# Fewer w4 products in the early attention units, output tiles seven units behind, sums by DMA for all but one unit

## The chip, the cores and the metric

The kernel runs on one core of a Trainium2 chip. The metric is the device time of one execution in microseconds. The kernel before takes 199.26 us, the median of three runs (198.9 to 199.65). The engines are named as in the profile: PE multiplies matrices, DVE, ACT and POOL work elementwise, SP only issues DMAs (ACT and POOL can issue them too). Every engine, and every queue of DMA issues, works in its own order: what stands behind a waiting instruction waits with it.

## The reference

An input `x` of 2048 rows by 512 columns in bf16 is normalized by rows and goes two ways; the output is `x + s * g`.

```python
xn = _layernorm(x)
s = _A_ref(xn, A_wqkv, A_wo)      # attention: 32 heads of 16, each row sees itself and rows 2, 4, ... 14 before it
g = _silu(_B_ref(xn, B_w1, B_w2, B_w3, B_w4))
...
    x1 = x + hs                   # hs: gelu(layernorm(x) @ w1), shifted by rows in four groups of columns, @ w2
    h2 = _gelu(_layernorm(x1) @ w3) @ w4
    return x1 + h2
```

The attention's weights are a softmax over 8 logits; the kernel takes exponentials without a maximum, sums them, and divides the weighted values by the sums afterwards. `w3` is 512 by 1376 and `w4` 1376 by 512.

## The kernel before

**Layout.** Since attention looks back by even distances, even and odd rows never meet there; they are two parities `p` of 1024 rows each. Until about 104 us the kernel normalizes, forms queries and keys, and does w1, w2 and w3. What is left is the *attention part*, which the change is about. There PE has four kinds of work:

- 17 *attention units*: unit 0 for the first 64 rows of both parities, then eight units of 120 rows for each parity. `scores(n)` (line 603) fills four PSUM banks, `exps(n)` (L614, ACT) takes exponentials, `within(n)` (L623, DVE) masks them in place, `values(n)` (L582) makes the value rows of the unit in the bank called b, which ACT copies (L587), and `weighted(n)` (L650) multiplies masked exponentials by values, with a column of constants that yields the sums. Its two banks o are emptied by DVE at the edge between the unit's two halves (`mix` L666, L667) and by ACT for the rest (L668), into a tile `orw`.
- 16 *w4 tiles* of 128 rows, `w4_part` (L529), 11 products each into the one bank w, then an add of x1 on DVE (L537) that also frees the bank.
- Gates: silu of a w4 tile, as `tanh` of half of it (ACT, L555, same function table as the exponentials) and a multiply (`gate_mult`, DVE, L561). At the end, after the last exponentials, ACT loads the table of silu and takes it directly (L547); such tiles are scaled by 2 later (`twice`), which is what the tanh form leaves in.
- 16 *output tiles* of 128 rows, `final(p, i)` (L802): attention rows `oT` by wo into a bank, DVE multiplies by the gate (L813, or L811 for tiles in `twice`), POOL adds x (L818), and SP stores two tiles at once (L844).

**Sums.** Units form *runs* that share the division. A run of two units spans 240 rows. `sums_gather` reads the sums out of `orw` by two DMAs (L679), `sums_invert` takes the reciprocal on DVE (L757) and writes it to DRAM (L759), `sums_read` reads it back spread over rows (L765), `moves` copies the weighted values into `oT` by eight DMAs (L693), and `sums_apply` multiplies (L773). The constant NC is 3: the last four units are runs of their own. Unit 13 goes by DMA like the others, with its apply on POOL. Units 14, 15 and 16 go through PE instead: `sums_turn` transposes the sums (L703), `sums_inverse` takes the reciprocal on DVE (L711) and expands it in two ACT copies (L716), `sums_back` transposes back (L741), `sums_mult` multiplies (L750). For units 15 and 16 `rows` also brings the weighted values to `oT` by PE (L728) and ACT (L733).

**Order.** The order on each engine is the order of the source; nothing is reordered. In unit n (0 to 15) the loop issues scores(n), weighted(n-1), exps(n), the eviction, values(n+1), the gates of earlier tiles, the DMAs of the runs, the mask, w4 tile n, the output tile due and the applies due. Output tile (p, i) is due in unit 6 + 8p + i, up to (1, 1) in unit 15. Unit 15 takes six of the 11 products of its w4 tile (`CUT`). The end, written out by hand, holds unit 16, five products of w4 tile 15 and an identity product (L535), output tiles (1, 2) to (1, 7), and the sums of three units between them. Tiles (1, 6) and (1, 7) take their add of x on PE (`pe_add`, L835 and L838, ACT copies the result, L839); (1, 7) works in two halves, the last half stored from ACT's queue.

Tiles are handed out from pools: `orw` and the exponentials share six buffers, xo (x for the output) has four, and from unit 10 the space of the queries of parity 0 is cut into sixteen `slots`.

## Time and profile before

| what | value |
|---|---|
| median of three runs | 199.26 us (198.9 to 199.65) |
| the profiled run | 199.36 us |
| its span | 197.6 us (197.64) |
| granted PE clock | 1.0 throughout |
| PE, ACT, DVE, POOL busy | 190.2, 126.7, 125.1, 61.8 us |
| attention part | from 103.3 us to the end |
| scores of unit 1 | 108.28 us |
| one unit, 1 to 5 | 4.32 us |
| one unit with an output tile, 6 to 14 | 5.18 us and some tenths in places |
| output tile (1, 7) begins | 191.96 us |
| last store issued by SP | from 193.10 us on |

The profile shows one execution. The span runs from the first instruction to the last; the device time lies a little above it. "The chain that ended last" follows the work back from the last instruction to what released each step. In the timeline a row gives start and length in us, the engine, the line of the kernel, and what was made from what; a bracket gives the time for which the engine was idle ahead of it and what ended that. Starts are what to compare on ACT and DVE, since the shown lengths of neighbours overlap by some 0.1 us.

### The profile page before, as it was taken

The numbers are of one execution on the slowest core, as the hardware profiler recorded it, in microseconds if no ns is written. First come the engines' busy times: TensorE is split into PE (matmuls) and PEld (weight loads), VectorE is DVE, ScalarE is ACT, GpSimd is POOL, SyncE is SP. The second block draws the span as 40 slices with busy tenths as digits, with TensorE's granted clock in tenths as the row PEclk, the third lists the DMA queues.
The fourth block names the chain that finished last, engine by engine and source line by source line (L and its number), as shares of the span: only waits on it lengthen the run. The fifth ranks groups of instructions, "written<-read, shape, count | busy, mean of one in ns | idle before, by whom it ended". The sixth has DMA issues, their size and how long they took to land.

```text
span 197.6 us, 6164 instructions
## 1 busy us (share of the span) xinstructions
PE 190.2 (96%) x2591; PEld 98.5 (50%) x2591; DVE 125.1 (63%) x249; ACT 126.7 (64%) x140; POOL 61.8 (31%) x114
## 2 busy tenths in 40 slices
PE   7699999999999999999999999999999999999991
PEld 2588844444444444444444555555555554546550
DVE  4788856418539968200004776788888887786892
ACT  3559849644830643556558788887666676667961
POOL 4135722810200220200000533032626242469760
PEclk9999999999999999999999999999999999999999
DMA  5982181389452256460330012222232271713333
GB/s 158 304 281 84 60 268 53 122 151 339 140 154 62 76 137 167 121 140 0 119 117 3 12 22 66 73 49 69 44 101 62 59 207 31 233 33 88 88 119 108
DMA packets 33643, 22.32 MB, mean 113 GB/s; under 512 B 17584, under 2 KB 33104, under 8 KB 33616
## 3 DMA queue, kind: packets, MB, share of 16 engines
q1 hardware_dynamic: 32256, 21.06, 37.5%
q0 software_dynamic: 1216, 0.81, 2.1%
q8 instruction: 20, 0.33, 0.7%
q10 hardware_dynamic: 144, 0.07, 0.1%
q14 instruction: 7, 0.06, 0.1%
HBM read 12.41 MB, written 4.83 MB: 87 GB/s over the span
## 4 chain that ended last, share of the span: by engine, by line
PE 91%; DMA 3%; DVE 2%; SPq 1%; issue 1%; ACT 1%; DVEq 0%
PE w_ps L529 19%; PE w_ps L394 18%; PE qk_ps L297 13%; PE v_ps L582 8%; PE w_ps L354 7%; PE w_ps L330 7%; PE wo_ps L802 6%; PE o_ps L650 6%; DMA wqk_sb<-in_A_wqkv_dram 3%; PE s_ps L603 3%; PE w_ps L410 1%; PE tr_ps L265 1%; SPq L118 1%; PE dt_ps L703 1%; DVE oT L750 1%
## 5 line engine op out<-in xcount | busy, mean ns | idle before, releaser
L614 ACT ACTIVATE prob<-s_ps 128x2048 bf16<-128x2048 f32 (+1 forms) x18 | 31.9, 1781 | 18.0 <-PE s_ps L603 17.9
L529 PE MATMUL w_ps<-w_sb,h3T 128*128 128x512 bf16 (+1 forms) x176 | 40.8, 379 | 0.0
L398 ACT ACTIVATE h3T<-w_ps 128x1024 bf16<-128x1024 f32 x20 | 20.5, 1023 | 24.9 <-PE w_ps L394 24.9
L693 POOL DMA_DIRECT2D oT<-orw x38 | 19.4, 518 | 49.9 <-DVE orw L658 30.3
L394 PE MATMUL w_ps<-x1nT,w_sb 128*128 128x512 bf16 x160 | 35.0, 379 | 0.0
L297 PE MATMUL qk_ps<-xnT,wqk_sb 128*128 128x256 bf16 (+1 forms) x192 | 29.7, 308 | 1.2 <-DMA wqk_sb<-in_A_wqkv_dram 0.7
L529 PEld LDWEIGHTS <-h3T 128*128 128x128 bf16 (+1 forms) x176 | 17.1, 98 | 20.4
L394 PEld LDWEIGHTS <-w_sb 128*128 128x128 bf16 x160 | 15.6, 98 | 19.1 <-issue 0.4
L297 PEld LDWEIGHTS <-wqk_sb 128*128 128x128 bf16 x192 | 18.3, 98 | 11.2 <-DMA wqk_sb<-in_A_wqkv_dram 1.0
L623 DVE TENSOR_TENSOR prob<-prob,band 128x2048 bf16<-128x2048 bf16 (+1 forms) x18 | 21.0, 1167 | 2.9 <-ACT prob L614 2.7
L304 ACT ACTIVATE qT<-qk_ps,sel 128x1024 bf16<-128x1024 f32 x16 | 16.7, 1113 | 6.6 <-PE qk_ps L297 6.5
L818 POOL TENSOR_TENSOR xo<-sg,xo 128x512 bf16<-128x512 bf16 x9 | 11.7, 1304 | 21.5 <-DVE sg L813 21.5
L802 PE MATMUL wo_ps<-wo_sb,oT 128*128 128x512 bf16 (+1 forms) x68 | 16.6, 366 | 0.1
L582 PE MATMUL v_ps<-wv_sb,xnT 128*128 128x512 bf16 x64 | 16.6, 381 | 0.0
L359 DVE TENSOR_TENSOR xn<-w_ps,xn 128x1024 bf16<-128x1024 f32 x8 | 9.7, 1212 | 10.6 <-PE w_ps L354 10.6
L537 DVE TENSOR_TENSOR xn<-w_ps,xn 128x512 bf16<-128x512 f32 x15 | 10.4, 691 | 7.6 <-PE w_ps L529 7.5
L585 DVE CAST v_aug<-v_ps 128x512 bf16<-128x512 f32 x1 | 0.7, 691 | 22.5 <-ACT h3T L398 22.5
L668 ACT ACTIVATE orw<-o_ps 128x896 bf16<-128x896 f32 x16 | 14.6, 913 | 0.1
L330 PE MATMUL w_ps<-xn2T,w_sb 128*128 128x512 bf16 x64 | 14.5, 379 | 0.0
L354 PE MATMUL w_ps<-w_sb,hT 128*128 128x512 bf16 x64 | 14.3, 379 | 0.0
L650 PE MATMUL o_ps<-prob,v_aug 64*32 64x64 bf16 x1088 | 12.2, 195 | 0.1
L334 ACT ACTIVATE hT<-w_ps 128x1024 bf16<-128x1024 f32 x8 | 8.2, 1028 | 6.2 <-PE w_ps L330 6.2
(100 smaller groups left out, 236.0 us busy)
## 6 DMA issues: line engine op xcount, KB each, us to landing
x1n_dram<-xn SPq DMA_DIRECT2D x4, 512.0 KB
xn<-in_A_x_dram SPq DMA_DIRECT2D x6, 256.0 KB
xo<-in_A_x_dram SPq DMA_DIRECT2D x6, 256.0 KB
out_dram<-xo SPq DMA_DIRECT2D x6, 256.0 KB
orw<-rden_d SPq DMA_DIRECT2D x6, 240.0 KB
w_sb<-in_B_w_dram SPq DMA_DIRECT2D x1, 1376.0 KB
w_sb<-in_B_w_dram SPq DMA_DIRECT2D x1, 1280.0 KB
wqk_sb<-in_A_wqkv_dram SPq DMA_DIRECT2D x2, 512.0 KB
```

What stands on the lines that cost most here:

```text
L297: pe.matmul(pt[:, b, :], lhsT=wqk_sb[:, dt, nt * P : (nt + 1) * P], rhs=xnT[p][:, dt, ms], start=(dt == 0), stop=(dt == ND - 1),)
L330: pe.matmul(pt[:, b, :], lhsT=w1_sb[:, dt, g * P : (g + 1) * P], rhs=xn2T[:, dt, :], start=(dt == 0), stop=(dt == ND - 1),)
L354: pe.matmul(pt[:, j, :], lhsT=w2_src(p, g, m0), rhs=w2_sb[:, g, :], start=(g == 0), stop=(g == ND - 1),)
L394: pe.matmul(pt[:, b, :], lhsT=w3_sb[:, dt, ft * P : (ft + 1) * P], rhs=x1nT[:, dt, :], start=(dt == 0), stop=(dt == ND - 1),)
L398: act.activation(h3_tile(c)[:, 2 * a : 2 * a + 2, :], pt, AF.Gelu_apprx_tanh)
L529: pe.matmul(pt, lhsT=h3[c][:fs, ft, jj * P : (jj + 1) * P], rhs=w4_sb[:fs, ft, :], start=(ft == 0), stop=(ft == NF - 1 and t < NN - 2),)
L582: pe.matmul(vp, lhsT=xnT[p][:, dt, k0 : k0 + P], rhs=wv_sb[:, dt, :], start=first, stop=last)
L614: act.activation(pr[:, rs_], t[:, rs_], AF.Exp, scale=SCALE)
L623: dve.tensor_tensor(out=w, in0=w, in1=b.unsqueeze(1).to_broadcast([P, m, KB]), op=ALU.min)
L650: pe.matmul(op[32 * cg : 32 * cg + 32, s, g * KB : (g + 1) * KB], lhsT=va[KB * s : KB * s + KB, dt * 8 + h, :], rhs=pr[KB * s : KB * s + K ...
L693: queues[hh % len(queues)].dma_start(out=oT[p][DH * hh : DH * (hh + 1), :, q0 : q0 + nq], in_=w[32 * cg : 32 * cg + DH, ND * jj : ND * jj ...
L802: pe.matmul(pt, lhsT=oT[p][:, dt, i * P : (i + 1) * P], rhs=wo_sb[:, dt, cs], start=(dt == 0), stop=(dt == ND - 1),)
```

## The change

Runs are now (0), then pairs up to (13, 14), then 15 and 16 alone, ten in all; NC is gone. Units 13, 14 and 15 have their sums by the DMA way, unit 16 alone through PE.

The w4 work is laid out by a table `part`: unit 0 takes tile 0, units 1 to 3 take tiles 1 and 2 (7, then 4 + 3, then 8 products), units 4 to 6 take tiles 3 and 4 likewise, unit n from 7 to 15 takes tile n - 2. In units 2 and 5, which end one tile and begin another, the first part stands ahead of values. Tiles 14 and 15 are left to the end. Output tiles are due in unit 7 + 8p + i, so seven, (1, 1) to (1, 7), are left to the end. Up to unit 6 the reciprocals and the reading back stand behind the mask. The first two applies come in unit 6 instead of 5. In units from 8 on SP issues four and POOL two of the six early moves of a run, instead of three and three.

At the end, the eviction of unit 15 goes to DVE, one of the two gathers of unit 15 is issued by ACT, four tiles (12 to 15) get silu directly instead of two, and the gate of output tile (1, 4) goes `through`: ACT copies the product out of PSUM in fp32 and doubles it, POOL multiplies by the gate and adds x.

```diff
-    NC = 3
-    runs = [(0, 0)] + [(a, a + 1) for a in range(1, NN - NC - 1, 2)] + [(a, a) for a in range(NN - NC - 1, NN)]
+    runs = [(0, 0)] + [(a, a + 1) for a in range(1, NN - 2, 2)] + [(a, a) for a in range(NN - 2, NN)]
...
-    def weighted(n, first=lambda: None):
+    def weighted(n, eng=act):
...
-        return lambda: act.activation(wide(ow, c, KB, m), wide(ov_, 0, CH + W, m), AF.Copy)
+        dst, src = wide(ow, c, KB, m), wide(ov_, 0, CH + W, m)
+        return lambda: act.activation(dst, src, AF.Copy) if eng is act else eng.tensor_copy(out=dst, in_=src)
...
-    def sums_gather(i):
+    def sums_gather(i, queues=[sp]):
...
-            sp.dma_start(
+            queues[j % len(queues)].dma_start(
...
+        def through(eng):
+
+            (cs, pt), = pts
+            o = slot(2).rearrange("p a d -> p (a d)").bitcast(F32)
+            act.activation(o, pt, AF.Copy, scale=2.0 if t in twice else 1.0)
+            sg = slot()
+            eng.tensor_tensor(out=sg, in0=o, in1=g_i, op=ALU.mult)
+            eng.tensor_tensor(out=x_o, in0=sg, in1=x_o, op=ALU.add)
...
-    final_at = {n: divmod(n - 6, 8) for n in range(6, 16)}
-    CUT = 6
+    final_at = {n: divmod(n - 7, 8) for n in range(7, 16)}
+    part = {0: [(0, 0, NF)]}
+    for n in (1, 4):
+        t = 1 + (n - 1) // 3 * 2
+        part.update({n: [(t, 0, 7)], n + 1: [(t, 7, NF), (t + 1, 0, 3)], n + 2: [(t + 1, 3, NF)]})
+    part.update({n: [(n - 2, 0, NF)] for n in range(7, NN - 1)})
     for i in range(0, 8, 2):
         load_xo(0, i)
     act.preload_act_table_set("exp_and_others")
     values(0)
     for n in range(NN - 1):
         scores(n)
-        back = [i for i, (a, b) in enumerate(runs) if b == n - 2 and i < R - NC]
+        back = [i for i, (a, b) in enumerate(runs) if b == n - 2]
         done = [i for i, (a, b) in enumerate(runs) if b == n - 1]
         evict = weighted(n - 1) if n > 0 else lambda: None
-        for i in back:
-            sums_invert(i)
+        if n > 6:
+            for i in back:
+                sums_invert(i)
         exps(n, 2 if n == 0 else 1)
-        if n == NN - 2:
+        evict()
+        gate_mult()
+        if len(part[n]) > 1:
+            w4_part(*part[n][0])
+        if n > 0:
             values(n + 1)
-        evict()
-        if 0 < n < NN - 2:
-            values(n + 1)
-        gate_mult()
         if n < NN - 2:
             gate_tanh()
         for i in done:
-            if i < R - NC:
-                sums_gather(i)
+            sums_gather(i)
         if n == 2:
             moves(0, [sp, pool], 1)
-        for i in back:
-            if 0 < i < R - NC - 1:
-                moves(i, [sp], None, [6, 7])
-            sums_read(i)
+        def read_back():
+            for i in back:
+                if i > 0:
+                    moves(i, [sp], None, [6, 7])
+                sums_read(i)
+        if n > 6:
+            read_back()
         for i in done:
             if i == 0:
                 moves(i, [sp, pool], 0)
-            elif i < R - NC - 1:
-                moves(i, [pool, sp], None, range(6))
-            elif i == R - NC - 1:
-                moves(i, [pool], None, range(4))
+            elif i == R - 3:
+                moves(i, [pool, sp])
             else:
-                moves(i, [pool, sp])
-        if n == NN - 2:
-            store(sp, 0, 6)
+                moves(i, [pool, sp] if n < 8 else [pool, sp, sp], None, range(6))
         within(n, 2 if n == 0 else 1)
-        late = [i for i, (a, b) in enumerate(runs) if n == max(b + 3, 5)]
-        w4_part(n, 0, NF if n < NN - 2 else CUT)
+        if n <= 6:
+            for i in back:
+                sums_invert(i)
+            read_back()
+        late = [i for i, (a, b) in enumerate(runs) if n == max(b + 3, 6)]
+        w4_part(*part[n][-1])
         if n == 0:
             values(n + 1)
         gate = final(*final_at[n]) if n in final_at else None
-        if n == NN - 2:
-            banks["end"] = True
-            sums_turn(R - 3, "o")
-            sums_inverse(R - 3)
-            for i in late:
-                sums_apply(i)
         if gate:
             gate(pool)
-        if n < NN - 2:
-            for i in late:
-                sums_apply(i)
-        if n == NN - 3:
-            moves(R - NC - 1, [pool], None, range(4, 8))
-        if n % 2 == 0 and 10 <= n < NN - 3:
-            load_xo((n - 2) // 8, (n - 2) % 8)
-        if n - 1 in final_at and n % 2 == 0 and n < NN - 3:
-            p, i = final_at[n - 1]
-            store(sp, p, i - 1)
-        if n in (10, 12):
-            load_xo(1, n - 6)
+        for i in late:
+            sums_apply(i)
+        if n in (10, 12, 14):
+            store(sp, 0, n - 10)
+        if n in (8, 10):
+            load_xo(1, n - 4)
+        if n in (12, 14):
+            load_xo(1, n - 12)
+    banks["end"] = True
     scores(NN - 1)
-    evict = weighted(NN - 2)
-    store(sp, 1, 0)
+    evict = weighted(NN - 2, dve)
+    sums_invert(R - 3)
     exps(NN - 1)
     evict()
+    sums_gather(R - 2, [sp, act])
+    sums_read(R - 3)
+    moves(R - 2, [pool], None, range(6))
     act.preload_act_table_set("silu_and_others")
-    w4_part(NN - 2, CUT, NF)
+    within(NN - 1)
+    w4_part(NN - 3, 0, NF)
+    for t in (NN - 5, NN - 4):
+        gate_silu(t)
+    sums_invert(R - 2)
+    moves(R - 2, [sp], None, range(6, 8))
+    sums_read(R - 2)
+    store(sp, 0, 6)
+    gate1 = final(1, 1, "b")
+    gate1(pool)
+    store(sp, 1, 0)
+    evict = weighted(NN - 1)
+    evict()
+    gate_silu(NN - 3)
+    layout("high", f=1, g=1, h=1, i=1)
+    final(1, 2, "f")(pool)
+    final(1, 3, "h")(pool)
+    store(sp, 1, 2)
+    w4_part(NN - 2, 0, NF)
     gate_silu(NN - 2)
-    within(NN - 1)
-    gate2 = final(1, 2, "b")
-    layout("high", f=1, g=1, h=1, i=1)
-    sums_back(R - 3, "f")
-    gate3 = final(1, 3, "h")
-    sums_apply(R - 4, pool)
-    evict = weighted(NN - 1, first=lambda: gate2(pool))
-    evict()
-    sums_turn(R - 2, "g")
-    sums_inverse(R - 2, rows(R - 2, "i"), True)
-    gate3(pool)
-    store(sp, 1, 2)
-    gate4 = final(1, 4, "w")
-    sums_mult(R - 3)
+    sums_apply(R - 3)
     sums_turn(R - 1, "g")
-    sums_back(R - 2, "f")
-    sums_inverse(R - 1, rows(R - 1, "h"), True)
-    sums_mult(R - 2)
-    gate_silu(NN - 3)
-    gate5 = final(1, 5, "b")
-    gate4(pool)
+    sums_inverse(R - 1, rows(R - 1, "i"), True)
+    gate4 = final(1, 4, "b")
+    gate4.through(pool)
+    sums_back(R - 1, "g")
+    sums_mult(R - 1)
+    sums_apply(R - 2)
+    gate5 = final(1, 5, "f")
     gate5(pool)
     store(sp, 1, 4)
-    sums_back(R - 1, "i")
-    gate6 = final(1, 6, "g")
-    sums_mult(R - 1)
+    gate6 = final(1, 6, "h")
     halves = [slice(0, D // 2), slice(D // 2, D)]
     add6 = pe_add(1, 6, "o", slice(0, D))
     gate6(None)
-    gate7 = final(1, 7, "fw", lambda: add6(gate6.sg))
+    gate7 = final(1, 7, "bw", lambda: add6(gate6.sg))
     store(sp, 1, 6, 1)
-    add7 = pe_add(1, 7, "h", halves[0])
+    add7 = pe_add(1, 7, "i", halves[0])
     gate7.mult(0)
     add7(gate7.sg)
     store(sp, 1, 7, 1, halves[0])
```

In the first line of this last part, `n - 6` becomes `n - 7`. Lines that start with a space are the same in both.

More of the change, by code (lines that the diff above doesn't have):

```diff
@@ L663, in weighted @@
         )
-        first()
         mix = small.tile([P, 2 * ND, W], F32, name="mix", tag="mix")
@@ L826, in gate @@
                     gate.add(eng)
+        def through(eng):
[5 more added lines that the diff above has]
+            eng.tensor_tensor(out=x_o, in0=sg, in1=x_o, op=ALU.add)
+        gate.through = through
         gate.mult = lambda k: mult(k, *pts[k])
```

## The prediction

> **What bounds the kernel now.** I read the busy shares, then the 40 slices, then the chain of waits in order of time, then the timeline of the attention part (from 104 us) engine by engine.
>
> ```profile
> PE 190.2 (96%) x2591; PEld 98.5 (50%) x2591; DVE 125.1 (63%) x249; ACT 126.7 (64%) x140; POOL 61.8 (31%) x114
> ...
> PE   7699999999999999999999999999999999999991
> ...
> PE 91%; DMA 3%; DVE 2%; SPq 1%; issue 1%; ACT 1%; DVEq 0%
> ```
>
> PE is the bound; the chain is PE work back to back. So products moved from one unit to another cost nothing by themselves, products removed gain their length, and a wait put ahead of PE loses its length. One early unit in the chain (start, length):
>
> ```profile
> 112.59 0.36 PE s_ps L603 x32
> 112.95 0.61 PE o_ps L650 x64
> 113.56 0.97 PE v_ps L582 x4
> 114.53 2.38 PE w_ps L529 x11
> ```
>
> ACT in the next unit, from the timeline (start, length, what it ran):
>
> ```profile
> 117.37 1.88 ACT L614 ACTIVATE prob<-s_ps 128x2048 bf16<-128x2048 f32 x1 [0.61 <-PE s_ps L603]
> 119.15 0.91 ACT L668 ACTIVATE orw<-o_ps 128x896 bf16<-128x896 f32 x1
> 119.94 0.60 ACT L587 ACTIVATE v_aug<-v_ps 128x512 bf16<-128x512 f32 x1
> 120.42 0.64 ACT L555 ACTIVATE sig<-xn 128x512 bf16<-128x512 bf16 x1
> ```
>
> A unit lasts 4.32 on PE: scores 0.36, weighted 0.61, values 0.97, eleven w4 products 2.38 (0.216 each). ACT starts one thing 1.78, 0.79 and 0.48 us after the last, and the tanh takes some 0.55: 3.05 without a tanh, 3.60 with one. An output tile is 0.86 on PE. Then three places of the timeline near the end, a reciprocal that waits for gathered sums (idle time before it in brackets), the last work of POOL and DVE, and the last SP stores:
>
> ```profile
> 174.12 0.53 DVE L757 RECIPROCAL rb<-dn 128x60 bf16<-128x60 bf16 x1 [0.55 <-DMA dn<-orw]
> ...
> 190.80 2.27 POOL L818 TENSOR_TENSOR slots<-slots 128x512 bf16<-128x512 bf16 x2 [1.40 <-PE wo_ps L802]
> 191.25 0.65 DVE L750 TENSOR_TENSOR oT<-rr_ps,oT 128x480 bf16<-128x480 f32 x1
> ...
> 193.10 1.68 SPq L844 DMA_DIRECT2D out_dram<-slots  x3
> ```
>
> The last three SP stores are issued back to back from 193.10, when POOL has added tiles 4 and 5 (190.80 + 2.27); the span ends 4.54 later, at 197.64. The profiled run took 199.36 with a span of 197.64, so 1.72 lies outside; the median of the runs shown is 199.26, 0.10 below. All sums below are made against 197.64 and 199.36. A measurement of this kernel tells about 0.5%, 1.0 us, from no change.
>
> **Units 1 to 15.** Up to the scores of unit 16, PE did 160 w4 products and ten output tiles from 108.28 to 181.21; afterwards 143 and nine. That moves 17 x 0.216 + 0.86 = 4.53 behind this point, which is then reached at 176.68 if nothing waits.
>
> Does anything wait? The six early units now hold 22 products per three units: 1.94 + 7 x 0.216 = 3.45, 3.45 and 3.67. Over six units PE needs 21.1, ACT 6 x 3.05 + 4 x 0.55 = 20.5: it fits, barely. The mask (L623) follows the exponentials: these start 0.57 after the scores, take 1.88, the mask 1.22, so weighted products can start 3.75 after the scores, where PE comes to them at 3.45 + 0.36 = 3.81. In units 2 and 5 one tile ends and the next begins in the same PSUM bank, and the add that frees it (L537, 0.69) stands ahead of the mask on DVE: mix and edge until 1.6, gate 2.2, add 2.9, mask 4.1. PE waits some 0.1 for the bank and 0.2 for the mask. That is 0.5 over both. So unit 16 starts at 177.2. The later units are as before (5.18 each, final tiles shifted by one); SP's extra move in each run falls in a queue that issues some 7 of every 10.4 us. The sums of runs 0 and 1 are applied one unit later, and the first output tile, which needs them, moves one unit later too.
>
> **From the scores of unit 16, taken as 0.** Removed: two transposes of sums (L703: 0.41 and 0.54), two transposes back (0.21 each), one row product (0.33): 1.70 of PE, and the 0.44 that PE waited at 181.62 for a reciprocal that held the bank of weighted. Also gone are four ACT expansions and two reciprocals from PSUM, hidden before. Added: two reciprocals by DMA, an eviction on DVE, two silus instead of tanhs, one gate sent through ACT and POOL.
>
> PE: scores 0.36, weighted(15) to 0.97, w4 tile 14 to 3.35, output (1,1) to 4.21. DVE meanwhile, in its order, by the times of unit 12: gate 0.18, apply 0.79, mix 1.35, edge 1.61, reciprocal of run 7 at 1.75. Its sums are gathered from -1.94 to -0.76. Such a gather was found landed 2.42 after its last issue (160.53 to 162.95) or waited for until 3.25 (170.87 to 174.12, behind two loads and a store). I take the first: one store and one load stand ahead here. Then the new eviction: between 0.91 (the same shape on ACT) and 1.23 (128x1024 on DVE); by elements of the DVE row 1.08. It ends at 3.2 and the mask of unit 16 at 4.4, so weighted(16) starts at 4.45: 0.24 of PE waiting.
>
> After it: two output tiles to 6.8, w4 tile 15 with its identity product to 9.4, transpose of sums 9.8, rows 10.1, output 4 to 11.0, back at 11.0 (reciprocal 0.36 and two expansions 0.72 after the transpose), output 5 to 12.1. Output 6 waits for the sums of run 8 on DVE: rows copied 11.5, multiply 12.15, apply 12.45. It runs from 12.5 to 13.4, 0.45 late. The DMA way of run 8 from the eviction at 3.2: gather issues 0.6, landing 2.4, reciprocal and issue 0.75, write to read 1.5 (123.91 to 125.41) to 2.1 (153.37 to 155.46), read issue 0.65, landing 2.33 (183.31 to 185.64): 11.5 to 12.1, just in time. Before, output 6 ended at 191.51; now 177.2 + 13.4 = 190.6: **PE is 0.95 earlier**.
>
> The stores are another matter. Output 4 now goes ACT copy (0.6, from 11.35), POOL multiply, POOL add, and only then comes POOL's add of output 5. SP's store of both stands ahead of the last two SP stores, and SP issues in order. POOL's two adds at 190.80 took 1.14 each. The fp32 multiply is not in the trace: no less than 1.14 (one operand is wider), at most 2.3 (all of it by bytes); I take 1.14, the row with the same engine and element count. So 11.95 + 3 x 1.14 = 15.4. An add that met an all-SBUF DVE multiply for 0.49 us (162.15 on 161.99) took 1.49, 0.34 more; the apply of run 8 meets the multiply for 0.35: 0.25 more. The stores start at 15.7, which is 192.9: **0.2 before 193.10**, later than PE needs them. With the same 4.54 behind: span 197.4, time 199.1.
>
> The Trainium skill ("GPSIMD Engine Reference", Performance versus the Vector engine) counts some 2.6 cycles per element for two inputs whatever their type: an estimate of 1.11 us for 512, which would leave the sum as it is, where 2.3 would make it 200.3. [...]
>
> **Rivals.**
> - *The waits of the walk are not there.* The bank and mask waits (0.5) and that of weighted(16) (0.24) come from latencies of 0.05 to 0.3 us on each hop; without them and without the collision on POOL (0.25) the stores start 1.0 earlier than in my sum and PE ends 1.7 earlier than before. Time 198.1. For it: 0.95 of PE is saved even with the waits, and every hop was taken at its full row. Against: DVE and ACT are over 90% filled in the early units.
> - *The sums come late (slower).* Place: DVE's in-order queue at unit 16, where two reciprocals now wait for gathers ahead of an eviction, a mask and gates. Price: 0.75 if the gather of run 7 takes 3.25; it moves the eviction, the mask and all behind. The gather of run 8 at 3.25 adds 0.85, its write and read 0.5 to 1.1 (179.71 to 182.66 is the longest). Output 6 and all after it then come 0.75 + 1.6 later than my walk: time 199.36 - 0.95 + 2.4 = 200.8. It decides once the landings add 0.75 us (beyond that the stores no longer cover it), and the kernel is slower than before once they add 0.95. For it: DVE had one such wait before and has two now, in one unit, with the moves of two runs on the same queues. Against: most rows before found the gather landed.
> - *The early units are bound by ACT and DVE.* If every early unit waits for its mask as units 2 and 5 do, by 0.35: 2.1 in place of 0.5, time 200.7. For it: 20.5 of 21.1 us. Against: the walk finds the mask 0.06 ahead in the other four.
> - *POOL's fp32 multiply costs 2.3*: 200.3.
>
> **How the numbers follow.** Forecast 199.1, chance 0.36, its own range 198.6 to 199.8 (collision none to all three steps, waits by 0.3 either way). Waits absent, 198.1: 0.34. Sums late, 200.8: 0.19. Early units, 200.7: 0.07. POOL's multiply, 200.3: 0.04, half of it within 0.5%. Faster by over 0.5%: 0.34; within: 0.36 + 0.02 = 0.38; slower: 0.19 + 0.07 + 0.02 = 0.28. Range 197.7 to 200.9: it leaves out the lower end of the second case and the upper half of the two slow ones, under 0.2.
>
> **What would show it.** Right: scores of unit 16 at 177.2 (wrong if after 178); idle PE ahead of weighted in units 3 and 6 only; weighted(16) about 4.45 after the scores; output 6 starting after L773 and not after output 5; the last SP stores beginning when POOL ends, 0.7 us or more after the PE chain could have had them. Wrong: DVE idle before L757 for more than 1.2 us at unit 16 (sums late), a POOL multiply far from 1.14, or PE waiting for ACT in the early units.

## The result and the profile after

The changed kernel takes **201.76 us**, the median of five runs (200.73 to 202.16), beside 199.64 (198.9 to 199.88) for the kernel before on the same chip: the ratio is 1.0109, with a 95% interval of 1.0074 to 1.0144. It is slower, and it lies 0.9 above the upper end of the range. The profiled run took 201.87 with a span of 200.2 at a granted clock of 0.999. Two runs in a slower state, one of e3_mid_light below and one of the kernel before beside it, are left out of the medians and ratios.

The page of the changed kernel, engines and their busy time first, then PE by slices, then the chain that ended last:

```profile
PE 190.5 (95%) x2559; PEld 97.1 (49%) x2559; DVE 125.1 (63%) x246; ACT 124.8 (62%) x135; POOL 59.3 (30%) x109
...
PE   7899999999999999999999999999899999999972
...
PE 76%; DMA 8%; SPq 5%; DVE 5%; issue 3%; ACT 1%; DVEq 0%; ACTq 0%
```

32 instructions went from PE, as meant, and its busy time stayed. But the chain is no longer PE back to back: 8% of it is DMA landings and 5% SP's issuing, and the slices of PE show an 8 past the middle, where before there were nines to the end.

Where the time went can be read from three points of each timeline: the start of scores(0), that of scores(16), and the issue of the last SP stores (the span ends 4.2 to 4.6 after it wherever SP issues all three, but for one kernel below, 5.2). By PE's work alone scores(0) to scores(16) should have taken 77.04 - 4.53 - 0.41 = 72.1: the kernel before took 77.04, and the products moved (4.53) and the 0.41 that unit 14's transpose of sums took ahead of scores(16) leave it.

| profiled run | scores(0) at | to scores(16) | of it units 7, 8 | scores(16) to last SP stores | span |
|---|---|---|---|---|---|
| before | 104.50 | 77.04 | 10.41 | 11.56 | 197.6 |
| predicted | 104.5 | 72.7 | 10.4 | 15.7 | 197.4 |
| changed | 104.04 | 75.16 | 12.47 | 16.58 | 200.2 |

So 2.5 us more than predicted passed ahead of scores(16), 2.1 of them in units 7 and 8, and 0.9 more behind it.

**Units 7 and 8.** The timeline of the changed kernel: the eviction of unit 4, the reciprocal of run 2 (units 3 and 4), then the stretch around its apply; start, length, engine, line, and in brackets the idle time before and what ended it:

```profile
124.83 0.94 ACT L668 ACTIVATE orw<-o_ps 128x896 bf16<-128x896 f32 x1
...
130.75 0.53 DVE L757 RECIPROCAL rb<-dn 128x60 bf16<-128x60 bf16 x1 [0.75 <-DMA dn<-orw]
...
136.00 0.69 DVE L813 TENSOR_TENSOR sg<-wo_ps,xn 128x512 bf16<-128x512 f32 x1 [0.45 <-PE wo_ps L802]
...
138.91 0.66 DVE L773 TENSOR_TENSOR oT<-oT,orw 128x960 bf16<-128x960 bf16 x1 [2.21 <-DMA oT<-orw]
139.48 0.22 DVE L665 COPY mix<-o_ps 128x64 f32<-128x64 f32 x1
139.73 0.23 DVE L666 TENSOR_TENSOR orw<-o_ps,mix 128x64 bf16<-128x64 f32 x1
...
140.04 0.92 ACT L668 ACTIVATE orw<-o_ps 128x896 bf16<-128x896 f32 x1 [1.72 <-DVE orw L666]
...
140.86 0.59 ACT L587 ACTIVATE v_aug<-v_ps 128x512 bf16<-128x512 f32 x1
...
141.50 0.81 PE L802 MATMUL wo_ps<-wo_sb,oT 128*128 128x512 bf16 x3 [0.96 <-ACT v_aug L587]
```

The apply stands last in unit 7, and DVE idles 2.21 ahead of it. (The bracket names a move, but those of run 2 were all issued by 133.73, and their semaphores were last set at 135.10; that of the reading back was last set at 138.69, so this is what came last.) Behind it in DVE's queue stand mix and edge of unit 8; ACT's eviction waits 1.72 for the edge, the copy of the values stands behind the eviction, and PE waits 0.96 for the bank that this copy frees. No engine ahead of PE is full; four in-order queues hand one late landing on to PE. Unit 7 had lost 0.73 before that (5.91 for 5.18): PE stalled for 0.27 inside its weighted products with nothing to wait for, and DVE, late by the 0.75 that run 2's reciprocal waited, had the applies of runs 0 and 1 (1.26) to do ahead of mix, so that output tile 0 began some 0.3 late. SP's queue in the same stretch shows why it is late (L679 gather, L693 moves, L759 the reciprocals' write, L765 the reading back):

```profile
123.49 0.52 SPq L759 DMA_DIRECT2D rden_d<-rb  x1
124.05 1.91 SPq L693 DMA_DIRECT2D oT<-orw  x2
126.43 0.65 SPq L765 DMA_DIRECT2D orw<-rden_d  x1
127.17 1.17 SPq L679 DMA_DIRECT2D dn<-orw  x2
128.39 2.41 SPq L693 DMA_DIRECT2D oT<-orw  x3
131.30 0.32 SPq L759 DMA_DIRECT2D rden_d<-rb  x1
131.67 2.06 SPq L693 DMA_DIRECT2D oT<-orw  x2
134.62 0.65 SPq L765 DMA_DIRECT2D orw<-rden_d  x1
```

The same steps in the kernel before, eviction, gather, reciprocal, write, reading back and apply:

```profile
127.91 0.91 ACT L668 ACTIVATE orw<-o_ps 128x896 bf16<-128x896 f32 x1
128.84 1.17 SPq L679 DMA_DIRECT2D dn<-orw  x2
132.19 0.52 DVE L757 RECIPROCAL rb<-dn 128x60 bf16<-128x60 bf16 x1
132.74 0.32 SPq L759 DMA_DIRECT2D rden_d<-rb  x1
134.57 0.65 SPq L765 DMA_DIRECT2D orw<-rden_d  x1
141.09 0.65 DVE L773 TENSOR_TENSOR oT<-oT,orw 128x960 bf16<-128x960 bf16 x1
```

In the changed kernel unit 4 was evicted at 125.77, but SP was issuing two moves of run 1 until 125.96 and then stood at its reading back until 127.08, which needs the write issued at 123.49. Run 2's gather went out at 127.17, 1.40 after the eviction (0.02 before the change). Its reciprocal started 3.58 later (3.35 before), its reading back 3.32 after the write (1.83 before), and that landed, by its semaphore, at 138.69, 4.07 after its issue (before the change at 138.01, 3.44 after). Eviction to data: 12.9 us, 9.2 before. And the apply's turn on DVE came 10.9 after the eviction, at 136.70, where it was 12.3 before, since the light units are shorter. Before, the data were 3.1 ahead of their apply; now they are 2.0 behind.

**The end.** From the same timeline:

```profile
192.22 1.15 POOL L834 TENSOR_TENSOR slots<-slots,xn 128x512 bf16<-128x512 f32 x1 [2.57 <-ACT slots L832]
192.31 1.32 DVE L773 TENSOR_TENSOR oT<-oT,orw 128x480 bf16<-128x480 bf16 x1
193.45 1.20 POOL L835 TENSOR_TENSOR slots<-slots 128x512 bf16<-128x512 bf16 x1
...
193.69 1.04 PE L802 MATMUL wo_ps<-wo_sb,oT 128*128 128x512 bf16 x4 [1.20 <-DVE oT L773]
194.61 1.15 POOL L818 TENSOR_TENSOR slots<-slots 128x512 bf16<-128x512 bf16 x1
...
195.78 1.59 SPq L854 DMA_DIRECT2D out_dram<-slots  x3
```

The apply of run 8 (128x480) took 1.32, as long as POOL's multiply stands, and PE idles 1.20 for it ahead of output 6. The SP stores start at 195.78, when POOL has done its third operation in a row, as the prediction's sum had it, only later. Some of that lateness has nothing to do with sums or stores: PE stalled in the weighted products of unit 15, with nothing that the profile shows to wait for.

```profile
180.41 0.43 PE L650 MATMUL o_ps<-prob,v_aug 64*32 64x64 bf16 x34 [0.46 <-issue]
```

### The profile page after: what moved, and what is told of

It reads as the page before. It is cut to its first block, busy times and chain, and to the rows that moved or that the text cites. A ratio compares the mean times of both kernels' runs of the same rounds, so it can differ in the third digit from the quotient of the medians.

```text
span 200.2 us, 6085 instructions
## 1 busy us (share of the span) xinstructions
PE 190.5 (95%) x2559; PEld 97.1 (49%) x2559; DVE 125.1 (63%) x246; ACT 124.8 (62%) x135; POOL 59.3 (30%) x109
## 4 chain that ended last, share of the span: by engine, by line
PE 76%; DMA 8%; SPq 5%; DVE 5%; issue 3%; ACT 1%; DVEq 0%; ACTq 0%
PE w_ps L394 17%; PE qk_ps L297 13%; PE w_ps L529 12%; PE w_ps L354 7%; PE w_ps L330 7%; PE wo_ps L802 6%; PE v_ps L582 4%; PE o_ps L650 4%; DMA wqk_sb<-in_A_wqkv_dram 3%; DMA oT<-orw 2%; DMA rden_d<-rb 2%; PE s_ps L603 2%; SPq L679 2%; DVE oT L773 2%; PE w_ps L410 1%
## 5 line engine op out<-in xcount | busy, mean ns | idle before, releaser
L614 ACT ACTIVATE prob<-s_ps 128x2048 bf16<-128x2048 f32 (+1 forms) x18 | 32.0, 1782 | 15.7 <-PE s_ps L603 15.6
L529 PE MATMUL w_ps<-w_sb,h3T 128*128 128x512 bf16 (+1 forms) x176 | 41.3, 379 | 0.4 <-DVE xn L537 0.4
L693 POOL DMA_DIRECT2D oT<-orw x33 | 16.9, 519 | 55.1 <-DVE orw L658 30.3
L802 PE MATMUL wo_ps<-wo_sb,oT 128*128 128x512 bf16 (+1 forms) x68 | 16.4, 366 | 2.5 <-DVE oT L773 1.2
L668 ACT ACTIVATE orw<-o_ps 128x896 bf16<-128x896 f32 x15 | 13.7, 914 | 2.7 <-DVE orw L666 2.7
L330 PE MATMUL w_ps<-xn2T,w_sb 128*128 128x512 bf16 x64 | 14.5, 379 | 0.0
L650 PE MATMUL o_ps<-prob,v_aug 64*32 64x64 bf16 x1088 | 12.9, 195 | 0.8 <-issue 0.7
```

Source lines behind the costliest of these rows:

```text
L330: pe.matmul(pt[:, b, :], lhsT=w1_sb[:, dt, g * P : (g + 1) * P], rhs=xn2T[:, dt, :], start=(dt == 0), stop=(dt == ND - 1),)
L529: pe.matmul(pt, lhsT=h3[c][:fs, ft, jj * P : (jj + 1) * P], rhs=w4_sb[:fs, ft, :], start=(ft == 0), stop=(ft == NF - 1 and t < NN - 2),)
L614: act.activation(pr[:, rs_], t[:, rs_], AF.Exp, scale=SCALE)
L650: pe.matmul(op[32 * cg : 32 * cg + 32, s, g * KB : (g + 1) * KB], lhsT=va[KB * s : KB * s + KB, dt * 8 + h, :], rhs=pr[KB * s : KB * s + K ...
L693: queues[hh % len(queues)].dma_start(out=oT[p][DH * hh : DH * (hh + 1), :, q0 : q0 + nq], in_=w[32 * cg : 32 * cg + DH, ND * jj : ND * jj ...
L802: pe.matmul(pt, lhsT=oT[p][:, dt, i * P : (i + 1) * P], rhs=wo_sb[:, dt, cs], start=(dt == 0), stop=(dt == ND - 1),)
```

## The experiments

Each kernel is the changed one with the edit shown. The first theory: SP's queue makes run 2 late and DVE's order passes that to PE (2.1), and POOL's multiply blocks DVE at the end (0.9). Rivals: the early units are full of their own work; the end is late by its transfers anyway. Thirteen kernels, in four groups, each group beside runs of the kernel before (medians 199.27, 199.04, 199.25 and 199.36). Ratios are to these runs; they are not quotients of the medians.

| kernel | scores(0) to (16) | units 7, 8 | to last SP stores | median us | ratio, 95% interval |
|---|---|---|---|---|---|
| e1_late2 | 74.02 | 10.76 | 16.13 | 200.87 | 1.0091 (1.0060 to 1.0122) |
| e2_pool_moves | 74.01 | 11.65 | 16.32 | 200.67 | 1.0073 (1.0038 to 1.0107) |
| e3_mid_light | 75.10 | 10.16 (light) | 16.06 | 202.14 | 1.0133 (1.0078 to 1.0188) |
| e4_through_dve | 74.96 | 12.25 | 16.34 | 201.85 | 1.0133 (1.0079 to 1.0186) |
| e5_relief | 74.94 | 12.40 | 16.05 | 201.88 | 1.0139 (1.0104 to 1.0175) |
| e6_end | 74.87 | 12.17 | 15.90, one from POOL | 202.68 | 1.0173 (1.0140 to 1.0207) |
| e7_pe15 | 74.37 | 11.86 | 17.13 | 201.92 | 1.0138 (1.0101 to 1.0175) |
| e8_both | 74.31 | 12.00 | 15.90, one from POOL | 203.70 | 1.0229 (1.0196 to 1.0262) |
| e9_shift2 | 74.84 | 11.72 | 15.97 | 200.67 | 1.0076 (1.0045 to 1.0107) |
| e10_end2 | 74.83 | 11.96 | 16.29 | 201.39 | 1.0091 (1.0068 to 1.0114) |
| e11_shift_end | 73.44 | 10.47 | 16.65 | 200.63 | 1.0075 (1.0048 to 1.0102) |
| e12_shift1 | 73.10 | 10.39 | 16.69 | 199.63 | 1.0010 (0.9987 to 1.0033) |
| e13_shift1_end | 73.14 | 10.49 | 16.04 | 199.97 | 1.0020 (0.9996 to 1.0044) |

How far such a profile can be trusted: the changed kernel, e4, e6, e7 and e10 have the same code up to scores(16), and took 75.16, 74.96, 74.87, 74.37 and 74.83. So a difference under 0.8 says nothing here. The changed kernel, e1, e2, e3, e5, e9 and e12 have the same code from scores(16) on, and their last stores begin 15.97 to 16.69 after it: there a difference under 0.7 says nothing.

### Run 2's apply one unit later (e1_late2)

```diff
-        late = [i for i, (a, b) in enumerate(runs) if n == max(b + 3, 6)]
+        late = [i for i, (a, b) in enumerate(runs) if n == (8 if b == 4 else max(b + 3, 6))]
```

> The changed kernel with one edit: the sums of run 2 are applied at the end of unit 8 instead of unit 7 (the first output tile that needs them is due in unit 9). Theory S (sums late: the apply of run 2 stands in DVE's queue until 138.91 for data read back at 134.62, and the mix, the eviction, the copy of values and so the output tile of unit 8 stand behind it): the DVE wait of 2.2 us ahead of L773 in unit 7 goes, and with it PE's 0.96 ahead of the output tile at 141.50 and some 0.3 around it; unit 8 falls from 6.56 to about 5.2 and the time by 1.2 to 1.5. Theory C (the early units are simply full on ACT and DVE): nothing changes, within 0.3.

DVE's wait before the apply went. Up to scores(16) the profile took 74.02, which is 1.1 less than the changed kernel's but only 0.35 less than that of e7, with the same early code, and the intervals of the times overlap (1.0060 to 1.0122 against 1.0074 to 1.0144): that the wait went is shown, a gain in time is not. The next wait showed; the changed kernel with this edit, DVE's timeline:

```profile
139.52 0.53 DVE L757 RECIPROCAL rb<-dn 128x60 bf16<-128x60 bf16 x1 [1.53 <-DMA oT<-orw]
```

Run 3's reciprocal waited for its gather, which SP had issued at 135.60 behind the reading back of run 2 (134.87); the bracket names a move of the same queue. So with the apply out of the way the lateness goes on to run 3; the late reading back stayed.

### The moves of runs 1 and 2 all from POOL (e2_pool_moves)

```diff
-                moves(i, [pool, sp] if n < 8 else [pool, sp, sp], None, range(6))
+                moves(i, [pool] if n < 6 else [pool, sp] if n < 8 else [pool, sp, sp], None, range(8 if n < 6 else 6))
...
-                if i > 0:
+                if i > 2:
                     moves(i, [sp], None, [6, 7])
```

> The changed kernel with one edit: all eight moves of runs 1 and 2 are issued by POOL, which has little to do before unit 7, and none by SP. SP then has two gathers, a write and a read for each of these runs, 2.2 us instead of 7. Theory S in the form that SP's queue in order is what makes the sums late: the gather of run 2 is issued at 125.8, when its eviction ends, instead of 127.17, its reciprocal waits no longer (0.75 before), the read-back is issued near 132 instead of 134.62, the apply in unit 7 waits under 0.3 instead of 2.2, and the time falls by 1.5 to 2. If the lateness is that of the landings alone (write to read 2.4, read to landing 3.6), the read-back comes at most 1 us earlier and the time falls by 0.5 or less. Theory C: no change.

About the same numbers as e1, by another way and as little clear of the changed kernel's: the reading back of run 2 was issued at 134.04 instead of 134.62, and DVE still idled 1.41 before the apply. SP's moves are a small part of the lateness: the gather of run 2 stood behind the reading back of run 1, at 126.80, without any move between them.

### The light units in the middle (e3_mid_light)

Units 1 to 6 keep a full w4 tile, units 7 to 12 take the light pattern.

```diff
-    for n in (1, 4):
-        t = 1 + (n - 1) // 3 * 2
+    part.update({n: [(n, 0, NF)] for n in range(1, 7)})
+    for n in (7, 10):
+        t = 7 + (n - 7) // 3 * 2
...
-    part.update({n: [(n - 2, 0, NF)] for n in range(7, NN - 1)})
+    part.update({n: [(n - 2, 0, NF)] for n in range(13, NN - 1)})
```

> The changed kernel with the light units elsewhere: units 1 to 6 take a whole w4 tile each, as in the kernel before, and units 7 to 12 take four tiles between them (7, 4 + 3, 8 products). PE's work is the same. Theory S: the time from the eviction of a run to its apply is again two units of 4.3, PE waits for no apply in units 6 to 9, and unit 16 begins 2.2 to 2.6 earlier than in the changed kernel (at 176.7 to 177.1 instead of 179.27). Theory C holds that a unit lighter than ACT and DVE can fill is the loss, wherever it lies: with an output tile these units are 4.4 on PE and DVE has 3.9 in them, so it also expects a gain, but the waits would be for the mask. What tells them apart is which wait is left in units 1 to 6: none by S.

Units 1 to 6 took 4.31 to 4.48 again, with no waits on PE, and units 7 to 12 took 4.77 to 5.18 where PE's work is 4.31 to 4.53. PE in this kernel:

```profile
138.78 1.02 PE L802 MATMUL wo_ps<-wo_sb,oT 128*128 128x512 bf16 x4 [0.51 <-ACT v_aug L587]
...
143.31 0.81 PE L529 MATMUL w_ps<-w_sb,h3T 128*128 128x512 bf16 x3 [0.57 <-DVE xn L537]
```

So here something near the prediction's third rival holds, though the wait is not for the mask, as both that rival and theory C had it: a light unit with an output tile waits for the add that frees the w4 bank, and for ACT's copy. The 2.2 to 2.6 that theory S expected were not won: where the light units stand changes which wait is met, not the sum.

### Output 4's gate on DVE in its place (e4_through_dve)

```diff
-    gate4.through(pool)
+    gate4.through(dve)
```

> The changed kernel with one edit: the multiply and the add of output tile (1, 4) behind ACT's copy are done by DVE, not POOL. Theory P (POOL and DVE exclude each other: the apply of run 8 started 0.09 after POOL's multiply at 192.22 and ended 0.26 after it, 1.32 instead of some 0.4, and output tile (1, 6) with it): the apply takes 0.35 to 0.45. DVE has 1.0 more to do, so output tile (1, 6) begins within 0.4 of before and the time stays within 0.5. If the 1.32 comes from something else (landing of the sums, DMA traffic), the apply still takes over 1 us and the time grows by 0.5 to 1.

DVE's timeline of this kernel:

```profile
191.69 0.69 DVE L834 TENSOR_TENSOR slots<-slots,xn 128x512 bf16<-128x512 f32 x1 [1.73 <-ACT slots L832]
192.41 0.42 DVE L835 TENSOR_TENSOR slots<-slots 128x512 bf16<-128x512 bf16 x1
192.76 0.65 DVE L750 TENSOR_TENSOR oT<-rr_ps,oT 128x480 bf16<-128x480 f32 x1
193.32 0.40 DVE L773 TENSOR_TENSOR oT<-oT,orw 128x480 bf16<-128x480 bf16 x1
```

The same apply takes 0.40 without POOL beside it and 1.32 with it: the block is shown. In e12_shift1 (below) it began 0.61 after POOL's multiply (190.76 and 190.15), took 0.80, and ended 0.26 after it, as in the changed kernel. The time did not move, since DVE now has 1.0 of work ahead of the apply.

### Both reliefs of the early sums (e5_relief)

The edits of e1 and e2 together, and the moves of run 0 from POOL too.

```diff
-            moves(0, [sp, pool], 1)
+            moves(0, [pool], 1)
...
-                moves(i, [sp, pool], 0)
+                moves(i, [pool], 0)
```

> Both reliefs of the early sums together: the apply of run 2 in unit 8 instead of 7, and the moves of runs 0, 1 and 2 all issued from POOL, none from SP. By the theory that the 2.1 us of units 7 and 8 come from SP's in-order queue and from DVE's in-order queue that hands the late apply on to PE: no idle DVE of over 0.5 before apply(2), gather(2) and read(2) issued 2 to 4 us earlier than in the changed kernel, and from scores(0) to scores(16) 73.0 to 73.3 (75.16 in the changed kernel, 74.0 with either relief alone). By the rival that the read-back's own landing bounds the sums, whoever issues the moves: 74.0 again, with recip(3) waiting for its gather as with the first relief alone. By the rival that the early units are bound by their own work: 74.0 or more, the lost time spread over units 1 to 9. End unchanged; time 199.9 to 200.3 by the first, 200.7 to 200.9 by the others.

Missed: 74.94. With SP free of moves, the reading back of run 1 still waited for its write (123.33 to 126.86), the gather of run 2 went out at 127.57 and let the reciprocal go only 3.2 after its last issue (2.4 in the changed kernel), beside eight moves from POOL. DVE waited there instead:

```profile
131.93 0.53 DVE L757 RECIPROCAL rb<-dn 128x60 bf16<-128x60 bf16 x1 [1.84 <-DMA dn<-orw]
```

(The end, too, cost it some: its stores were issued 16.05 after scores(16), but the span ended 5.2 after them.) Of the three expectations the last, "74.0 or more", holds the number, but not its sign: the loss is not spread over units 1 to 9, unit 7 alone took 7.10. So "SP's moves" fell as the cause. What is left is the length of the chain itself, eviction, gather, reciprocal, write, reading back, apply, against the time that the light units leave for it; whichever step is late, DVE's order hands it on.

### The end with output 4's gate behind the apply (e6_end, e8_both)

```diff
-    gate4.through(pool)
...
     gate5 = final(1, 5, "f")
+    gate4(pool)
     gate5(pool)
-    store(sp, 1, 4)
+    store(pool, 1, 4)
```

> Only the end differs from the changed kernel: output 4's gate multiply back on DVE from PSUM and placed behind apply(8), its add on POOL, and its second store issued from POOL. By the theory that POOL's multiply held DVE off for 0.9 us inside apply(8): apply(8) takes 0.41 to 0.5, output 6's matmuls begin 0.6 to 0.9 earlier (13.5 to 13.8 after scores(16), 14.4 before this edit), the time is 0.5 to 1.0 shorter: 200.8 to 201.3. By the rival that the sums of run 8 come late anyway, by its write and read: apply(8) is short but waits for the read, output 6 gains under 0.3 and the time under 0.3. From scores(0) to scores(16) 75.1 to 75.2 in both.

The second kernel has this and the edits of e5.

> The reliefs of the early sums and the edit of the end together. If the two losses are separate places on the one path of PE, the gains add: 1.9 to 2.1 from scores(0) to scores(16) and 0.5 to 1.0 at the end, time 198.8 to 199.6, level with the kernel before. If the end only absorbs what the early units give (it waits for transfers that do not come earlier), the gain is that of the early reliefs alone, 199.9 to 200.3.

Output 6 began 13.0 after scores(16), 1.4 earlier than in the changed kernel, 0.46 of it by the stall in unit 15 that only the changed kernel's profile has in that size, and the apply of run 8 took 0.40. But the time did not fall, and e8_both, at 203.70, lies above both its expectations and is the slowest of all. POOL's store was issued at 195.31 and the span ended 5.1 later (in e8_both at 195.08, 6.7 later), while three SP stores mostly end 4.2 to 4.6 after their first. With the store back on SP's queue (e10_end2, below) the same kernel takes 1.3 less, 1.0068 to 1.0114 against 1.0140 to 1.0207: the issue from POOL ate the gain.

### Unit 15's sums through PE again (e7_pe15)

No gather, write, reading back or moves for unit 15; two transposes and the rows through PE, as before the change.

```diff
-    sums_gather(R - 2, [sp, act])
-    moves(R - 2, [pool], None, range(6))
-    sums_invert(R - 2)
-    moves(R - 2, [sp], None, range(6, 8))
-    sums_read(R - 2)
...
+    sums_turn(R - 2, "g")
+    sums_inverse(R - 2, rows(R - 2, "i"), True)
     w4_part(NN - 2, 0, NF)
     gate_silu(NN - 2)
+    sums_back(R - 2, "g")
     sums_apply(R - 3)
-    sums_turn(R - 1, "g")
+    sums_mult(R - 2)
+    sums_turn(R - 1, "f")
...
-    sums_apply(R - 2)
```

> One part undone: the sums and rows of unit 15 go through PE again as in the kernel before, with no gather, write, read or moves by DMA for it. By the theory that the end is late by DMA landings and by POOL's lock on DVE: PE gets 0.95 more work, apply(7)'s wait (0.88) and most of the wait before output 6 (1.2) go, the time is 200.9 to 201.9 (0 to 0.9 shorter than the changed kernel). By the rival that PE's own work bounds the end and that waits there are only the order's slack: 0.7 to 0.95 longer, 202.4 to 202.7. From scores(0) to scores(16) 75.1 to 75.2 in both.

PE's waits in the end went and its last product came 16.4 after scores(16) instead of 17.1, in spite of some 1.0 more work. The stores did not follow: POOL's multiply and two adds ran from 191.84 to 195.34, and SP's stores began at 195.36. The time is that of the changed kernel. So taking unit 15's sums off PE, over half of the 1.70 that the change saves there, is worth nothing here, since what ends last is ACT's copy, POOL's three steps, and the stores.

### All of run 2 later, applied in unit 9 (e9_shift2, e11_shift_end)

```diff
-        back = [i for i, (a, b) in enumerate(runs) if b == n - 2]
+        back = [i for i, (a, b) in enumerate(runs) if n == (7 if b == 4 else b + 2)]
...
-        late = [i for i, (a, b) in enumerate(runs) if n == max(b + 3, 6)]
+        late = [i for i, (a, b) in enumerate(runs) if n == (9 if b == 4 else max(b + 3, 6))]
```

In these two kernels output tile 2 is multiplied by wo before run 2 is divided by its sums, so that part of the computation is left out of it; the instructions are the same.

> Every step of run 2's sums from the reciprocal on is one to two units later: reciprocal, write and read in unit 7 instead of 6, ahead of unit 7's exponentials, and the apply in unit 9 instead of 7. Nothing else is changed; queues and moves are those of the changed kernel. By the theory that the chain of four landings takes about 13 us whoever issues it, that three light units give it only 11, and that DVE's in-order queue hands whichever step is late (reciprocal or apply) on to PE: no DVE idle of over 0.5 that ends by a landing in units 6 to 9, units 7 and 8 together 10.4 to 10.8 (12.5 in the changed kernel), scores(0) to scores(16) 73.0 to 73.5, time 199.8 to 200.4. By the rival that the wait goes on to the next run as it did with the apply alone put off: run 3's reciprocal or apply idles DVE by over 1, scores(0) to scores(16) 74.0, time 200.7. By the rival that the light units are bound by ACT and DVE work anyhow: 74.5 or more.

The second has this and the end of e10_end2.

> Both together: run 2's later sums and the end with the multiply on DVE. If the two losses lie one behind the other on PE's path, the gains add: scores(0) to scores(16) 73.0 to 73.5, end 20.1 to 20.4 after scores(16), time 199.1 to 199.7, level with the kernel before and not past it. If the end waits for what the early units do not move: 199.8 to 200.4. If neither holds: 201.5 to 202.

e11_shift_end: units 7 and 8 took 10.47 and scores(16) came after 73.44, as expected; the two applies at the end of unit 9 cost PE 0.45 in unit 10. So the early units did as the theory said, but the time did not: 200.63 lies in none of the three expected ranges, and 1.0 above e12_shift1 below, whose profile is only 0.3 shorter up to scores(16). Why is open. In e9_shift2 (74.84, outside its range) the same code lost 1.2 elsewhere, in the middle of the weighted products of unit 7:

```profile
131.96 0.24 PE L650 MATMUL o_ps<-prob,v_aug 64*32 64x64 bf16 x12 [1.22 <-issue]
```

"issue" means that nothing in the profile held PE. The end in e11_shift_end was no shorter: its apply of run 8 was short (0.41) but waited 0.54 for the reading back, 13.2 after scores(16).

### The end with the gate on DVE and SP's store (e10_end2)

The edit of e6, with `store(sp, 1, 4)` kept.

> The end as in the kernel with output 4's gate multiply on DVE behind apply(8), but with its second store back on SP's queue. By the theory that POOL's lock cost 0.9 in apply(8) and that issuing a store from POOL ate the gain there: output 6's matmuls begin 13.0 to 13.3 after scores(16) as with that kernel, the last store is issued by 17.4 after scores(16) (18.1 in the changed kernel), the end comes 20.1 to 20.4 after scores(16) (20.95 in the changed kernel), the time is 0.5 to 0.8 shorter than the changed kernel, 201.0 to 201.3. By the rival that DVE's own queue bounds the end, now with one 0.68 multiply more: end 20.9 to 21.2 after scores(16), time 201.8 to 202.1.

Output 6 at 13.3, the stores at 16.29 (inside the 15.97 to 16.69 of the unedited end), the time 0.4 below the changed kernel's, with intervals that overlap (1.0068 to 1.0114 against 1.0074 to 1.0144). POOL's adds now wait for DVE's gate behind the apply, so what PE gained the stores lost again. Here, too, PE stalled 1.21 on "issue" in unit 7, and run 2's apply met no wait: the stall had given its data the time. (It took 1.63 all the same, begun 0.03 after an add on POOL at 138.03.)

### Run 2's reciprocal, write, reading back and apply one unit later (e12_shift1, e13_shift1_end)

```diff
-        back = [i for i, (a, b) in enumerate(runs) if b == n - 2]
+        back = [i for i, (a, b) in enumerate(runs) if n == (7 if b == 4 else b + 2)]
...
-        late = [i for i, (a, b) in enumerate(runs) if n == max(b + 3, 6)]
+        late = [i for i, (a, b) in enumerate(runs) if n == (8 if b == 4 else max(b + 3, 6))]
```

> Run 2's reciprocal, write and read one unit later (in unit 7, ahead of its exponentials) and its apply at the end of unit 8, still ahead of output 2. By the theory that the DMA chain of run 2 is longer than the light units and that DVE's order hands its lateness to PE: units 7 and 8 take 10.4 to 10.8 (12.5 in the changed kernel), no wait is left in units 9 to 15 since run 3's steps stay where they are, scores(0) to scores(16) 73.0 to 73.4, time 199.8 to 200.3; where PE stalls on its own issue in unit 7, as in two of the profiles, 1.2 more. By the rival that the waits only move on to run 3's steps: 74.0, time 200.7.

The second has the end of e10_end2 too.

> The same with output 4's gate multiply on DVE behind apply(8). By the theory that the two losses lie one behind the other: scores(0) to scores(16) 73.0 to 73.4 and the end 20.6 after scores(16) (20.95 in the changed kernel), time 199.4 to 200.0, still not past the kernel before, since 0.9 of the early units' own waits and about 0.5 of the end stay. By the rival that the end then waits for the stores behind POOL's adds, whatever comes earlier: end 21.0 to 21.3 after scores(16), time 199.8 to 200.6.

The expected numbers up to scores(16) held, and the time of e12_shift1 came out 0.2 below its range: units 7 and 8 took 10.39 and 10.49, as before the change (10.41), and scores(16) came after 73.10 and 73.14. DVE's timeline of e12_shift1, with the reciprocals of runs 2 and 3 and the apply of run 2:

```profile
131.88 0.52 DVE L757 RECIPROCAL rb<-dn 128x60 bf16<-128x60 bf16 x1
...
136.61 0.52 DVE L757 RECIPROCAL rb<-dn 128x60 bf16<-128x60 bf16 x1
...
140.81 0.65 DVE L773 TENSOR_TENSOR oT<-oT,orw 128x960 bf16<-128x960 bf16 x1
```

None of the three has a bracket. The time is 199.63, against 199.36 before: no measurable difference (0.9987 to 1.0033). Two changed conditions thus remove the whole loss, with the end untouched. They change SP's order too: run 3's gather now goes out ahead of run 2's reading back (133.06 and 135.93), where it stood behind it (135.37 and 134.62). How much is due to the later place and how much to this order was not tried; e1, which leaves the order, shows run 3's reciprocal waiting 1.53 for that gather. Of the later end e13_shift1_end shows 0.65 in its profile, within what the same end varies by, and nothing in its median (199.97, 1.0020, 0.9996 to 1.0044), which fits its theory and its rival alike: unclear. No version beat the kernel before.

## Why the prediction was wrong

**The step that failed** is this one: "SP's extra move in each run falls in a queue that issues some 7 of every 10.4 us. The sums of runs 0 and 1 are applied one unit later, and the first output tile, which needs them, moves one unit later too." It checked runs 0 and 1 and passed over run 2, whose apply stays in unit 7 while the units before it shrink. The light units were priced by the work of the engines alone. The chain of DMAs through them, counted in units by the source and in microseconds by the chip, was not followed for the early units at all. Its numbers stood in the trace of before: 9.2 from the eviction to the data, the apply at 12.3. With 1.3 less room and the chain 3.7 longer, by a gather behind another run's reading back (1.4), a reading back behind a slower write (1.5), and 0.9 in landings, 3.1 of slack became 2.0 of lateness. e12_shift1 shows the size: the median 2.1 lower than the changed kernel's, 199.63 beside a predicted 199.1. (0.27 of the loss in units 7 and 8 is the stall of PE, which e12_shift1 does not have either.)

The other steps in their order:

- *Products moved cost nothing where PE is the bound*: right. Without the late sums scores(0) to scores(16) is 73.1, 1.0 above PE's own work.
- *Waits in units 2 and 5, 0.25 each*: the place right, the size not. The starts of scores(2), (3), (5) and (6) (111.20, 115.12, 122.37, 126.27) give 3.92 and 3.90 for 3.45 of work, 0.46 each; the six early units lost 1.1 (0.9 in e12_shift1).
- *The rival that sums come late*: the right mechanism, DVE's in-order queue behind a late landing, at the wrong place. It was put at unit 16 and priced at 200.8; there the reciprocal of run 8 waited 0.53, no more than the 0.55 before. It struck at unit 7. A second place, the apply of run 7 in the end, waited 0.88, and 2.36 in e12_shift1, where PE lost 0.65 by it.
- *The rival of the early units*, 200.7: not the cause here. The six lost 1.1, where it said 2.1; e3_mid_light shows such a loss, by other waits than the mask, for light units that carry an output tile.
- *weighted(16) 4.45 after scores(16)*: 4.92 in the changed kernel's profile, 0.46 of it the stall of PE in unit 15. In the twelve kernels whose profile shows no such stall there (e10_end2 has one of 0.17) it came at 4.38 to 4.49: the step is right. The eviction on DVE took 1.03 (1.08 estimated).
- *Run 8 by DMA just in time, 11.5 to 12.1*: 0.8 to 1.6 late. Where the apply waited for its data, it began at 12.9 (e3_mid_light) to 13.7 (e12_shift1). In the changed kernel the reading back was issued 3.4 after the write, not 1.5 to 2.1, with two moves and other transfers between. Output 6 began at 14.5, not 12.5.
- *POOL's fp32 multiply 1.14*: 1.15, right, as long as the bf16 add (1.15); that rival (2.3) was wrong.
- *The collision, 0.25 on POOL*: the term was mis-sized and on the wrong engine. DVE's apply took 1.32 for 0.41 (e10_end2) or 0.40 (e4_through_dve). It began 0.09 after POOL's multiply and ended 0.26 after it: it did not share with POOL, it waited. The prediction had POOL pay, by the row in which an add took 1.49 for 1.14; there the DVE multiply had begun first, at 161.99 against 162.15. The Trainium skill ("SBUF — State Buffer", SBUF: two separate sides) has the rule that covers both: a GpSimd operation that reads SBUF and a DVE operation with two SBUF inputs lock the shared ports, whichever starts first, for its whole length. The traces agree but for some 0.1, by which 0.26 is less than the 0.40 of the apply alone: POOL had started first at 192.22, and the 128x960 apply, begun while POOL added three tiles, took 1.63 for 0.65.
- *The stores at 15.7, behind POOL*: 16.58, and what they wait for was right: POOL's third step. Output 4's copy began 1.0 later than in the sum (12.35 after scores(16), not 11.35), 0.46 of it by the stall; POOL's three steps followed without the collision's 0.25.

The sum of the misses, profiled run against forecast: 2.46 up to scores(16) (2.1 in units 7 and 8, some 0.6 in the early units, the rest of the other sign), 0.88 behind it, 0.12 less from the stores to the end, and 0.46 that scores(0) came earlier: 2.76, of the 2.77 between 201.87 and 199.1.

Still open: what the rest of the end's 0.9 is. With the 0.46 of the stall taken off, 0.4 is left, and the other six kernels with the same end lie 0.3 to 1.0 above the walk. No edit took it away; each moved the wait to the next step (DVE's order in e4, POOL's adds in e10, the reading back in e11). That PE's stall is a loss of this kernel and not of this profile is not shown. And with run 2 mended nothing is won: the PE work saved by the sums of unit 15 is not on the path that ends last (e7_pe15).

## What to carry to other kernels

When a stage is made shorter, follow every chain of transfers that spans it, landing by landing, and compare its length in microseconds with the new time to its consumer: the slack of the trace before is the number to spend, and here it was 3.1. A late landing is charged to the bound engine by in-order queues in between, so easing the queue that issues it may only move the wait to the next step; moving all its waiting steps one stage later took it away. And look for an elementwise POOL operation that begins just ahead of a DVE operation with two inputs in SBUF on the path.

## What the runs showed of the hardware that was not expected

- A DVE multiply of two SBUF tiles (128x480 bf16) took 0.40 to 0.41 alone, 1.32 beside a POOL multiply that had begun 0.09 earlier, and 0.80 beside one that had begun 0.61 earlier (e12_shift1).
- With a store of 256 KB issued from POOL the span ended 5.1 and 6.7 after its issue; where SP issues three, it ended 4.2 to 4.6 after the first (5.2 in e5_relief). In e6_end its packets ended at 197.74, 2.6 ahead of the span's end; in the changed kernel the last packets of the stores ended 1.7 ahead of it (198.43 of 200.15).
- PE stalled inside the weighted products with nothing to wait for: in unit 7 for 0.27 in the changed kernel, 1.22 in e9_shift2 and 1.21 in e10_end2, in unit 15 for 0.46 in the changed kernel and 0.17 in e10_end2. In the trace a 16 KB packet of the instruction queue ends at 129.78, 130.38 and 131.19 in the first three and at 179.00 and 178.86 in the last two, and PE goes on 1.41 to 1.58 later, at 131.24, 131.96, 132.76, 180.41 and 180.34. In e11_shift_end, with the early code of e9_shift2, that packet ended at 128.73 and there was no stall. That PE waited for its own instructions is argued from these times, and no experiment tried it.
